# The first 512 tokens loaded by feature blocks beside weight pieces, and the first 32 matmuls run block by block

## The chip, the cores and the metric

The kernel runs on one core of one Trainium2 chip. The metric is device time in microseconds; the median of three runs of the kernel before is 504.48 (504.27 to 505.07).

## The reference

Two attention branches share one input x (1 x 2048 x 1024, bf16). Each projects it with a weight wqkv (1024 x 3072) into q, k and v of 32 heads of 32, and its result with wo (1024 x 1024). Branch A is linear attention; branch B attends to 8 earlier tokens at distances 0, 2, ..., 14. A sigmoid gate mixes the two for each token:

```
x = A_x
g = sigmoid((x * gate_w).sum(-1))
a: q,k,v = x @ A_wqkv;  phi(t) = where(t > 0, t + 1, exp(t)) + 1e-6
   o = phi(q) (phi(k)^T v) / (phi(q) sum(phi(k)));   a = o @ A_wo
b: q,k,v = x @ B_wqkv;  o = softmax over 8 dilated positions;  b = o @ B_wo
out = g * a + (1 - g) * b
```

The change touches only the start of the first product, the values of branch B: v = x @ B_wqkv[:, 2048:3072].

## The kernel before, in words

Everything goes through a planner. `P.op` (L79) records an operation with its engine, an estimated cost, a priority and the tiles that it reads and writes. `schedule` (L120) orders each engine's queue by list scheduling with these costs, and `emit` (L202) writes the queues out with the semaphore waits that the tiles demand. `plan` (L1223) is run six times, each pass choosing the PSUM banks by the pass before. So the order on each engine is fixed before the chip runs, and each queue is worked strictly in that order.

x is kept transposed in SBUF as xT, 128 partitions x 8 feature blocks x 2048 tokens. `load_x` (L1292) brings one tile of 128 tokens with all 1024 features by a transposing DMA from SP's queue. `load_w` (L1297) brings rows of a weight half (512 columns), in pieces of one or more blocks of 128 rows.

The first stage computes branch B's values, which are the first useful work of the kernel. Its loads are issued in L1306 to L1314: tile 0 on SP; the first half's weights in four pieces of two row blocks, two from ScalarE's (ACT) queue and two from SP's; tiles 1, 2, 3; the second half's weights in four pieces; then the other tiles in between the stores. The loop at L1368 takes four tiles at a time, first with the first half of the weights, then with the second. For each tile and half, `group` (L1320) issues eight matmuls of 128x128 by 128x512 that sum over the features into one PSUM bank, out of seven that rotate; tile 0 does so in four steps of two blocks, each of which waits only for its own weight piece. `move` (L1352) copies the bank to SBUF on ACT or VectorE (DVE), and a store takes it to HBM (L1377). The stage has 256 matmuls; behind them come the gate's product (L1392), k and q of branch B, and the rest, all on TensorE (PE) in one queue.

Ahead of the first useful matmul stand warm-up matmuls (L1363) on a zeroed tile `warm` into the eighth bank. They use no input data. In the kernel before they are nine of 512 columns, and VectorE zeroes the tile (L1272). GpSimd (POOL) sets up the constants, ident first (L1252).

Of the kernel before, what the change touches and what calls it, by code (L numbers as in the profile page):

```python
# [9 lines left out]
BF16 = mybir.dt.bfloat16  # L10
# [1092 lines left out]
def build_kernel(nc, A_x, A_wqkv, A_wo, B_x, B_wqkv, B_wo, gate_w, out):  # L1103
    del B_x
    S = A_x.shape[1]
    NT = S // 128
    HS = S // 2
    x2 = A_x[0].rearrange("(m e) d -> e m d", e=2)
# [5 lines left out]
    def SB(shape, dtype, name, at=None):  # L1114
        n = SZ[dtype]
        for d in shape[1:]:
            n *= d
        if at is None:
            at = base[0]
            base[0] += (n + 31) // 32 * 32  # L1120
        uid[0] += 1
        h = nc.alloc_sbuf_tensor_at("%s_%d" % (name, uid[0]), list(shape), dtype, offset=at)
        return Tile("S", h, at, list(shape), dtype)
# [28 lines left out]
    banks = [Bank(i) for i in range(8)]  # L1152
# [6 lines left out]
    def hb(p0, p1, half):  # L1159
        return [("H%d" % half, p0, p1, None)]  # L1160

    xT = SB([128, 8, S], BF16, "xT")
    qT = SB([128, 8, S], BF16, "qT")
    kT = SB([128, 8, S], BF16, "kT")
    ws = [SB([128, 8, 1024], BF16, "w%d" % i) for i in range(4)]
# [16 lines left out]
    mx4 = SB([128, 4], F32, "mx4")  # L1182
    mx1 = SB([1, 4], F32, "mx1")
    flag = SB([1, 1], I32, "flag")
    warm = SB([128, 512], BF16, "warm")
    er = Ring([SB([128, 512], BF16, "e%d" % i) for i in range(3)])

    ph = base[0]
# [25 lines left out]

    FILL = 0.2
    PVLAG = 3
    WARM = 9
    PASSES = 6
    mm = lambda n: max(n / 2400.0, 0.0267) + 0.0025
    act = lambda n: 0.19 + n / 1200.0  # L1220
    dps = lambda n: 0.14 + n / 960.0

    def plan(seen):  # L1223

        P = Prog(nc, nc.alloc_semaphore)
# [23 lines left out]
        def C(eng, fn, cost, writes, reads=()):  # L1249
            return P.op(eng, fn, cost, reads=reads, writes=writes, prio=-1)  # L1250

        C("pool", lambda e: e.memset(ident[:], 0.0), 0.2, [ident.all()])  # L1252
        C("pool", lambda e: e.affine_select(out=ident[:], in_=ident[:], compare_op=ALU.not_equal, fill=1.0, base=0,
                                            pattern=[[-1, 128]], channel_multiplier=1), 0.3, [ident.all()], [ident.all()])
# [14 lines left out]
        C("pool", lambda e: e.memset(kvbd[:], 0.0), 0.9, [kvbd.all()])  # L1269
        C("pool", lambda e: e.memset(zbd[:], 0.0), 0.9, [zbd.all()])  # L1270

        C("dve", lambda e: e.memset(warm[:, :], 0.0), 0.15, [warm.all()])  # L1272
        for m in mx[0:2]:
            C("dve", lambda e, m=m: e.memset(m[:, :], 0.0), 0.2, [m.all()])

# [12 lines left out]
        Bw = B_wqkv.rearrange("(dc p) f -> p dc f", p=128)  # L1288
# [3 lines left out]
        def load_x(t, prio):  # L1292
            e_, r = t // 8, t % 8
            return P.op("sp", lambda e: e.dma_start_transpose(xT[:, :, t * 128:(t + 1) * 128], x2[e_, r * 128:(r + 1) * 128, :]),  # L1294
                        1.5, writes=[xT.part((0, 8), (t * 128, (t + 1) * 128))], prio=prio, chan="x%d" % t, lat=1.3)

        def load_w(slot, half, src, c0, prio, d0=0, d1=8, eng="sp", after=()):  # L1297
            n = d1 - d0
            return P.op(eng, lambda e: e.dma_start(ws[slot][:, d0:d1, half * 512:half * 512 + 512], src[:, d0:d1, c0:c0 + 512]), 0.4 + 0.2 * n,  # L1299
                        writes=[ws[slot].part((d0, d1), (half * 512, half * 512 + 512))], prio=prio, chan="w%d_%d_%d" % (slot, half, d0), lat=0.55 * n, after=after)  # L1300
# [2 lines left out]
            with nc.allow_non_contiguous_dma(reason="tiny gate_w transposed load"):  # L1303
                return e.dma_start(gw[:, :], gate_w.rearrange("(dc p) -> p dc", p=128))

        load_x(0, 0)  # L1306
        load_w(0, 0, Bw, 2048, 0.1, 0, 2, "act")
        load_w(0, 0, Bw, 2048, 0.2, 2, 4, "act")
        load_w(0, 0, Bw, 2048, 0.3, 4, 6)
        load_w(0, 0, Bw, 2048, 0.4, 6, 8)  # L1310
        for t in range(1, NT):
            load_x(t, 3 + t)
        for d in range(0, 8, 2):
            load_w(0, 1, Bw, 2560, 6.1 + 0.1 * d, d, d + 2)  # L1314
# [3 lines left out]
        main = Pool(banks[0:7])  # L1318

        def group(bank, lhs, rhs, reads, lo=0, hi=8):  # L1320
            def fn(e):
                last = None
                for dc in range(lo, hi):
                    last = e.matmul(bank.ap(), lhs(dc), rhs(dc), start=(dc == 0), stop=(dc == 7))  # L1324
                return last
            return P.op("pe", fn, (hi - lo) * mm(512), reads=reads, writes=[bank.iv])
# [13 lines left out]
        def x_tile(t):  # L1340
            return (lambda dc: xT[:, dc, t * 128:(t + 1) * 128]), xT.part((0, 8), (t * 128, (t + 1) * 128))

        def x_chunk(u):
            return (lambda dc: xT[:, dc, u * 512:(u + 1) * 512]), xT.part((0, 8), (u * 512, (u + 1) * 512))

        def w_half(slot, half):
            return (lambda dc: ws[slot][:, dc, half * 512:half * 512 + 512]), ws[slot].part((0, 8), (half * 512, half * 512 + 512))

        def w_cols(slot, j):
            return (lambda dc: ws[slot][:, dc, j * 128:(j + 1) * 128]), ws[slot].part((0, 8), (j * 128, (j + 1) * 128))  # L1350

        def move(dst, src, n, bank, reg, scale=None, reads=()):  # L1352

            if scale is None:
                fd = lambda e: e.tensor_copy(dst, src())  # L1355
                fa = lambda e: e.activation(dst, src(), ACT.Copy)  # L1356
            else:
                fd = lambda e: e.tensor_scalar(dst, src(), scale, None, op0=ALU.mult)
                fa = lambda e: e.activation(dst, src(), ACT.Copy, scale=scale)  # L1359
            P.op("any", {"act": fa, "dve": fd}, {"act": act(n) + (0.1 if reads else 0.0), "dve": dps(n)}, reads=[bank.iv] + list(reads), writes=[reg])  # L1360

        for i in range(WARM):
            P.op("pe", lambda e: e.matmul(banks[7].ap(), warm[:, 0:128], warm[:, :], start=True, stop=True), 0.43, reads=[warm.all()], writes=[banks[7].iv], prio=-1)  # L1363


        early = {(2, 0): (1, 0, Bw, 1024, 21), (4, 1): (2, 0, Bw, 0, 22), (7, 1): (1, 1, Bw, 1536, 23), (10, 1): (2, 1, Bw, 512, 24),
                 (12, 1): (3, 0, Aw, 1024, 25), (14, 1): (3, 1, Aw, 1536, 26)}
        for t, half in [(4 * b + i, half) for b in range(NT // 4) for half in range(2) for i in range(4)]:  # L1368
            vt, vs = vst.next()
            xs, xr = x_tile(t)  # L1370
            bank = main.next()
            w, wr = w_half(0, half)
            step = 2 if t == 0 else 8
            for d in range(0, 8, step):
                o = group(bank, xs, w, [xr, ws[0].part((d, d + step), (half * 512, half * 512 + 512))], d, d + step)
            move(vt[:, :], bank.ap, 512, bank, vt.all())
            P.op("sp", lambda e, t=t, vt=vt, half=half: e.dma_start(vB_hbm[t * 128:(t + 1) * 128, half * 512:half * 512 + 512], vt[:, :]), 0.6, reads=[vt.all()],  # L1377
                 writes=[hb(t * 128, (t + 1) * 128, half)], chan="vst%d" % vs, lat=0.5, prio=5)
            if (t, half) in early:
                load_w(*early[t, half], after=[o])  # L1380
# [28 lines left out]
        main = Pool(banks[0:4])  # L1409
# [78 lines left out]
        for e_ in range(2):  # L1488
            if True:
                for j in range(8):  # L1490
                    for isq in range(2):
                        for u in (2 * e_, 2 * e_ + 1):
                            bank = main.next()
                            w, wr = w_cols(1 + isq, j)
                            xs, xr = x_chunk(u)
# [37 lines left out]
        for t in range(NT):  # L1533
            pkt, _ = pk.next()
            azt, _ = az.next()
            xs, xr = x_tile(t)
            for r in range(4):
                bank = main.next()
                w, wr = w_half((3, 0)[r // 2], r % 2)
# [16 lines left out]
        main = Pool(banks)  # L1556
# [109 lines left out]
        for t in range(NT):  # L1666
# [4 lines left out]
            for f0, f1 in parts:  # L1671
                bank = main.next()
                n = f1 - f0

                def fn(e, t=t, bank=bank, f0=f0, f1=f1):
# [8 lines left out]
                    reads=[bank.iv, gm.all(), tgt.part((i0, i1), (c0, c0 + 128))], writes=[o_.part((f0, f1))])  # L1684
                if t == NT - 1 or f1 == 1024:
                    c = f0 if t == NT - 1 else 0
                    P.op("sp", lambda e, e_=e_, r=r, o_=o_, c=c, f1=f1: e.dma_start(out2[e_, r * 128:(r + 1) * 128, c:f1], o_[:, c:f1]), 0.5,
                         reads=[o_.part((c, f1))], chan="out%d_%d" % (os_, c), lat=1.0)
# [8 lines left out]
    for _ in range(PASSES):  # L1697
        got = plan(seen)
        seen = got[2]
        if best is None or got[0].span < best[0].span:  # L1700
            best = got
    P, flag_op = best[:2]
# [22 lines left out]
def bass_gated_mix__linear_attn_block__sliding_local_dilated__prompt_kernel(nc, A_x, A_wqkv, A_wo, B_x, B_wqkv, B_wo, gate_w, out):  # L1725
    return build_kernel(nc, A_x, A_wqkv, A_wo, B_x, B_wqkv, B_wo, gate_w, out)
# [28 lines left out]
```

## Time and profile before

| | |
|---|---|
| three runs | 505.07, 504.48, 504.27 us |
| span of the profiled execution | 502.5 us |
| median less that span | 1.98 us |
| PE busy | 488.5 us (97%) |
| first warm-up matmul, first useful matmul | 1.25 us, 6.08 us |
| gate's product begins | 62.11 us |
| x and weight loads in the first 11 us on SP | 0.80 to 10.65 us |

The span runs from the first to the last instruction of one profiled execution; the run's time is measured from outside and is longer. All times in the profile count from the start of the span. A row of the timeline gives start, length, engine, line, operation, output and input, the number of instructions merged, and in brackets the idle time before with what ended it. SPq and ACTq are the issues of DMAs on those engines' queues, which are not the transfers themselves; the time to landing is from the issue to the last piece of data. "PEld" is the weight load of a matmul. Stretch rows give, after the stretch and its length, the busy time of PE, PEld, DVE, ACT and POOL with counts, the granted clock, the mean share of the 16 DMA engines, and GB/s.

### The profile page before, as it was taken

To read this page: it belongs to the slowest core of one execution; us is meant where nothing else is said; L and a number is where in the kernel's file an instruction comes from. 1 tells how busy PE (TensorE), PEld (TensorE's weight loads), DVE (VectorE), ACT (ScalarE), POOL (GpSimd) and SP (SyncE) were. 2 spreads that over 40 slices of the span, in tenths; PEclk is the share of its full clock that TensorE was granted. 3 is DMA by queue.
4 is the path that set the end of the run, shared out by engine and by line. 5 is a ranking of instruction groups with operands and counts; after the bars stand their busy time and mean duration, and the time that the engine had idled before them with its cause. 6 is when DMAs were issued, how large, how long until landed. Compare 5 with 4: busy or idle time off the path is not lost.

```text
span 502.5 us, 11582 instructions
## 1 busy us (share of the span) xinstructions
PE 488.5 (97%) x5190; PEld 232.6 (46%) x5257; DVE 264.6 (53%) x456; ACT 192.9 (38%) x335; POOL 6.6 (1%) x30
## 2 busy tenths in 40 slices
PE   8999999999999999999999999999999999999996
PEld 2444444444454444544544545444444444444443
DVE  3112235556667676454555464678776563234443
ACT  1111111111354454655554555479864543100000
POOL 5000000000000000000000000000000000000000
PEclk9999999999999999999999999999999999999999
DMA  8999990000024060100010100500000000011222
GB/s 222 207 204 314 353 270 1 1 0 1 12 86 139 22 198 27 34 23 23 23 39 21 33 1 3 170 0 1 0 2 0 2 0 1 1 43 64 83 78 73
DMA packets 47410, 34.92 MB, mean 69 GB/s; under 512 B 22261, under 2 KB 43125, under 8 KB 47354
## 3 DMA queue, kind: packets, MB, share of 16 engines
q1 hardware_dynamic: 46810, 33.59, 23.6%
q8 instruction: 43, 0.70, 0.6%
q10 hardware_dynamic: 544, 0.52, 0.4%
q14 instruction: 13, 0.11, 0.1%
HBM read 21.51 MB, written 8.40 MB: 60 GB/s over the span
## 4 chain that ended last, share of the span: by engine, by line
PE 95%; issue 2%; DMA 1%; ACT 1%; SPq 0%; DVE 0%
PE ps_all L1324 76%; PE ps_all L1677 11%; PE ps_all L1427 2%; PE ps_all L1447 2%; PE ps_all L1602 1%; PE ps_all L1452 1%; PE ps_all L1523 1%; DMA xT<-in_A_x_dram 1%; PE ps_all L1580 1%; ACT ra L1604 0%; PE ps_all L1392 0%; SPq L1294 0%; SPq L1299 0%; ACT e L1333 0%; ACT ra L1605 0%
## 5 line engine op out<-in xcount | busy, mean ns | idle before, releaser
L1324 PE MATMUL ps_all<-w,xT 128*128 128x512 bf16 x922 | 207.8, 379 | 5.6 <-issue 4.0
L1324 PE MATMUL ps_all<-xT,w 128*128 128x512 bf16 x747 | 169.2, 379 | 2.5 <-issue 1.9
L1324 PEld LDWEIGHTS ps_all<-w,xT 128*128 128x128 bf16 x960 | 91.3, 98 | 110.3 <-issue 1.7
L1324 PEld LDWEIGHTS ps_all<-xT,w 128*128 128x128 bf16 x768 | 73.9, 98 | 88.8 <-ACT ra L1604 0.6
L1677 PE MATMUL ps_all<-w,qT 128*128 128x512 bf16 (+1 forms) x259 | 55.2, 373 | 0.3
L1677 PEld LDWEIGHTS ps_all<-w,qT 128*128 128x128 bf16 x264 | 25.8, 98 | 29.7
L1335 DVE TENSOR_SCALAR e<-e 128x512 bf16<-128x512 bf16 x64 | 18.4, 291 | 38.9 <-ACT e L1331 25.3
L1355 DVE CAST vst<-ps_all 128x512 bf16<-128x512 f32 x15 | 10.4, 691 | 42.7 <-PE ps_all L1324 42.7
L1433 ACT ACTIVATE E<-ps_all 128x1824 bf16<-128x1824 f32 (+1 forms) x18 | 30.4, 1687 | 3.1 <-PE ps_all L1427 2.0
L1331 ACT ACTIVATE e<-ps_all 128x512 bf16<-128x512 f32 x32 | 19.1, 597 | 31.6 <-PE ps_all L1324 30.8
L1333 ACT ACTIVATE e<-ps_all 128x512 bf16<-128x512 f32 x32 | 19.2, 601 | 29.3 <-PE ps_all L1324 27.8
L1681 DVE SCALAR_TENSOR_TENSOR o<-ps_all,gm,xT 128x512 bf16<-128x512 f32 (+1 forms) x25 | 18.2, 729 | 23.0 <-PE ps_all L1677 22.8
L1280 DVE TENSOR_TENSOR mx<-mx,kT 128x1024 bf16<-128x1024 bf16 x32 | 20.7, 688 | 16.9 <-ACT kT L1356 16.8
L1280 DVE TENSOR_TENSOR mx<-mx,qT 128x1024 bf16<-128x1024 bf16 x32 | 20.7, 688 | 16.7 <-ACT qT L1359 16.6
L1356 ACT ACTIVATE vst<-ps_all 128x512 bf16<-128x512 f32 x17 | 10.1, 597 | 47.8 <-PE ps_all L1324 47.8
L1436 DVE TENSOR_TENSOR E<-E,msk 128x1824 bf16<-128x1824 bf16 (+1 forms) x18 | 19.8, 1100 | 14.5 <-ACT E L1433 14.5
L1462 DVE TENSOR_TENSOR qT<-ps_all,L 128x456 bf16<-128x456 f32 (+1 forms) x36 | 21.1, 624 | 7.7 <-ACT L L1461 7.7
L1359 ACT ACTIVATE qT<-ps_all 128x512 bf16<-128x512 f32 x15 | 9.0, 597 | 37.0 <-PE ps_all L1324 37.0
L1337 DVE SCALAR_TENSOR_TENSOR pk<-ps_all,e 128x512 bf16<-128x512 f32 x32 | 22.0, 688 | 0.8
L1604 ACT ACTIVATE ra<-ps_all,eps 128x512 f32<-128x512 f32 x32 | 21.5, 688 | 2.2 <-PE ps_all L1602 2.0
L1356 ACT ACTIVATE az<-ps_all 128x512 bf16<-128x512 f32 x19 | 11.4, 600 | 27.6 <-PE ps_all L1324 27.6
L1356 ACT ACTIVATE kT<-ps_all 128x512 bf16<-128x512 f32 x14 | 8.4, 597 | 35.5 <-PE ps_all L1324 35.5
(77 smaller groups left out, 336.5 us busy)
## 6 DMA issues: line engine op xcount, KB each, us to landing
w<-in_A_wqkv_dram SPq DMA_DIRECT2D x6, 1024.0 KB, 8.2
v<-vB_hbm SPq DMA_DIRECT2D x36, 128.0 KB, 2.6
vB_hbm<-vst SPq DMA_DIRECT2D x32, 128.0 KB, 4.9
w<-in_B_wqkv_dram SPq DMA_DIRECT2D x4, 1024.0 KB, 8.3
out_dram<-o SPq DMA_DIRECT2D x15, 256.0 KB, 2.0
w<-in_A_wo_dram SPq DMA_DIRECT2D x2, 1024.0 KB, 5.6
w<-in_B_wo_dram SPq DMA_DIRECT2D x2, 1024.0 KB, 6.5
w<-in_B_wqkv_dram SPq DMA_DIRECT2D x6, 256.0 KB, 4.1
```

What stands on the lines that cost most here:

```text
L1280: P.op("dve", lambda e, m=m, op=op: e.tensor_tensor(m[:, 0:n], m[:, 0:n], src, op), 0.08 + n / 1920.0, reads=[m.all(), reg], writes=[m.all()],
L1324: last = e.matmul(bank.ap(), lhs(dc), rhs(dc), start=(dc == 0), stop=(dc == 7))
L1331: P.op("act", lambda e: e.activation(e_[:, :], bank.ap(), ACT.Exp), act(512), reads=[bank.iv], writes=[e_.all()])
L1333: P.op("act", lambda e: e.activation(e_[:, :], bank.ap(), ACT.Exp, accum_out=qe[:, col:col + 1]), act(512) + 0.1, reads=[bank.iv], writes= ...
L1335: P.op("dve", lambda e: e.tensor_scalar(e_[:, :], e_[:, :], 1.0, 1e-6, op0=ALU.min, op1=ALU.add), 0.25, reads=[e_.all()], writes=[e_.all()])
L1337: P.op("dve", lambda e: e.scalar_tensor_tensor(out=dst, in0=bank.ap(), scalar=0.0, in1=e_[:, :], op0=ALU.max, op1=ALU.add), dps(512), read ...
L1356: fa = lambda e: e.activation(dst, src(), ACT.Copy)
L1433: P.op("act", lambda e: e.activation(E[:, 0:32 * nq].rearrange("p (j q) -> p j q", j=4), ps[:, 4:8, 0:8 * nq], ACT.Exp), act(32 * nq), rea ...
L1436: P.op("dve", lambda e: e.tensor_tensor(ev(), ev(), m[:, :, :].rearrange("p r q -> p (r q)")[:, None, :].to_broadcast([128, 16, 2 * nq]), ...
L1462: P.op("dve", lambda e, L=L, pb=pb, g=g: e.tensor_tensor(qT[:, 4 * g:4 * g + 4, t0 + qs:t0 + qs + 2 * nq].rearrange("p c (h q) -> p h c q" ...
L1604: P.op("act", lambda e: e.activation(R[:, :], db.ap(), ACT.Ln, bias=eps[:, :]), act(512), reads=[db.iv, eps.all()], writes=[R.all()])
L1677: last = e.matmul(bank.ap(0, f1 - f0), qT[:, dc, t * 128:(t + 1) * 128], ws[3][:, dc, f0:f1], start=(dc == 0), stop=(dc == 7))
```

## The change

The first four tiles are no longer loaded one by one. Eight transposing DMAs on SP each bring one block of 128 features of all 512 tokens; eight weight pieces of one row block each go out on ACT's queue. The first 32 matmuls (four tiles, first weight half) run block by block: one matmul for each of the four tiles, into four banks, then the next block. Tiles from 4 on, the second half's weights and all later work are issued as before. The warm-up becomes 22 matmuls of 128 columns on a 128x128 tile, which POOL zeroes as its first operation.

```diff
-    warm = SB([128, 512], BF16, "warm")
+    warm = SB([128, 128], BF16, "warm")
-    WARM = 9
+    WARM = 22
+        C("pool", lambda e: e.memset(warm[:, :], 0.0), 0.2, [warm.all()])
         C("pool", lambda e: e.memset(ident[:], 0.0), 0.2, [ident.all()])
...
-        C("dve", lambda e: e.memset(warm[:, :], 0.0), 0.15, [warm.all()])
...
-        load_x(0, 0)
-        load_w(0, 0, Bw, 2048, 0.1, 0, 2, "act")
-        load_w(0, 0, Bw, 2048, 0.2, 2, 4, "act")
-        load_w(0, 0, Bw, 2048, 0.3, 4, 6)
-        load_w(0, 0, Bw, 2048, 0.4, 6, 8)
-        for t in range(1, NT):
+        for d in range(8):
+            P.op("sp", lambda e, d=d: e.dma_start_transpose(xT[:, d:d + 1, 0:512], x2[0, 0:512, d * 128:(d + 1) * 128]), 0.75,
+                 writes=[xT.part((d, d + 1), (0, 512))], prio=0.1 * d, chan="xd%d" % d, lat=0.4)
+            load_w(0, 0, Bw, 2048, 0.1 * d + 0.05, d, d + 1, "act")
+        for t in range(4, NT):
             load_x(t, 3 + t)
...
-            P.op("pe", lambda e: e.matmul(banks[7].ap(), warm[:, 0:128], warm[:, :], start=True, stop=True), 0.43, ...
+            P.op("pe", lambda e: e.matmul(banks[7].ap(0, 128), warm[:, :], warm[:, :], start=True, stop=True), 0.11, ...
...
+        first = [main.next() for _ in range(4)]
+        for d in range(8):
+            for t in range(4):
+                o = group(first[t], x_tile(t)[0], w_half(0, 0)[0],
+                          [xT.part((d, d + 1), (t * 128, t * 128 + 128)), ws[0].part((d, d + 1), (0, 512))], d, d + 1)
         for t, half in [(4 * b + i, half) for b in range(NT // 4) for half in range(2) for i in range(4)]:
             vt, vs = vst.next()
             xs, xr = x_tile(t)
-            bank = main.next()
             w, wr = w_half(0, half)
-            step = 2 if t == 0 else 8
-            for d in range(0, 8, step):
-                o = group(bank, xs, w, [xr, ws[0].part((d, d + step), (half * 512, half * 512 + 512))], d, d + step)
+            if t < 4 and half == 0:
+                bank = first[t]
+            else:
+                bank = main.next()
+                step = 2 if t == 0 else 8
+                for d in range(0, 8, step):
+                    o = group(bank, xs, w, [xr, ws[0].part((d, d + step), (half * 512, half * 512 + 512))], d, d + step)
```

More of the change, by code (lines that the diff above doesn't have):

```diff
@@ L1362, in plan @@
         for i in range(WARM):
-            P.op("pe", lambda e: e.matmul(banks[7].ap(), warm[:, 0:128], warm[:, :], start=True, stop=True), 0.43, reads=[warm.all()], writes=[banks[7].iv], prio=-1)
+            P.op("pe", lambda e: e.matmul(banks[7].ap(0, 128), warm[:, :], warm[:, :], start=True, stop=True), 0.11, reads=[warm.all()], writes=[banks[7].iv], prio=-1)
         early = {(2, 0): (1, 0, Bw, 1024, 21), (4, 1): (2, 0, Bw, 0, 22), (7, 1): (1, 1, Bw, 1536, 23), (10, 1): (2, 1, Bw, 512, 24),
                  (12, 1): (3, 0, Aw, 1024, 25), (14, 1): (3, 1, Aw, 1536, 26)}
+        first = [main.next() for _ in range(4)]
[3 more added lines that the diff above has]
+                          [xT.part((d, d + 1), (t * 128, t * 128 + 128)), ws[0].part((d, d + 1), (0, 512))], d, d + 1)
         for t, half in [(4 * b + i, half) for b in range(NT // 4) for half in range(2) for i in range(4)]:
```

## The prediction

> **What bounds the kernel now.** The page's first part comes first: which engine has no room. Its second row is the engines' busy time; the share of the chain by engine stands further down the page.
>
> ```profile
> span 502.5 us, 11582 instructions
> ...
> PE 488.5 (97%) x5190; PEld 232.6 (46%) x5257; DVE 264.6 (53%) x456; ACT 192.9 (38%) x335; POOL 6.6 (1%) x30
> ...
> PE 95%; issue 2%; DMA 1%; ACT 1%; SPq 0%; DVE 0%
> ```
>
> TensorE (PE) is the bound from end to end. Only its 14 us without work (502.5 - 488.5) can be had without taking matmuls away. The waits of PE alone say where they are, in total, times and longest:
>
> ```profile
> PE ps_all L1324 <- issue: 5.9, 37, 0.2
> PE ps_all L1363 <- DVE warm L1272: 1.3, 1, 1.3
> PE ps_all L1324 <- DMA xT<-in_A_x_dram: 1.0, 2, 0.8
> ```
>
> The 5.9 us are gaps of at most 0.2 us, spread over the kernel. The only data that PE waits for as a matmul is xT, at the very beginning. So the change can act only there, and the chain of waits and PE's timeline show that stretch (start, length, what):
>
> ```profile
> 0.80 1.37 SPq L1294
> 2.17 0.06 issue
> ...
> 3.35 4.94 DMA xT<-in_A_x_dram
> ...
> 8.33 7.16 PE ps_all L1324 x32
> ...
> 15.55 10.74 PE ps_all L1324 x49
> ...
> 62.11 1.84 PE ps_all L1392 x32
> ```
>
> ```profile
> 1.25 4.02 PE L1363 MATMUL ps_all<-warm 128*128 128x512 bf16 x9 [1.25 <-DVE warm L1272]
> 6.08 2.06 PE L1324 MATMUL ps_all<-w,xT 128*128 128x512 bf16 x8 [0.81 <-DMA xT<-in_A_x_dram]
> 8.33 8.03 PE L1324 MATMUL ps_all<-w,xT 128*128 128x512 bf16 x35 [0.18 <-DMA xT<-in_A_x_dram]
> ```
>
> Nine idle-data matmuls run from 1.25 to 5.27. The first useful matmul starts at 6.08, when token tile 0 has landed; its eight are through at 8.14, and tile 1 lets the ninth start at 8.33. From there PE runs on: 248 matmuls until the gate's line at 62.11, so (62.11 - 8.33) / 248 = 0.217 us each. By this rate the 32nd ends at 8.33 + 24 x 0.217 = 13.54 and the 40th at 15.27. **This is the yardstick: whatever the 40th gains, the whole kernel gains**, because in the built program PE's later instructions stand in the old order, and no wait for a DMA shows behind it. The profiled execution spans 502.5 us; the median of the runs shown, 504.48, is 1.98 more, which I carry over unchanged.
>
> **Part 1: the warm-up.** Rate and zeroing, by groups and timeline:
>
> ```profile
> L1363 PE MATMUL ps_all<-warm 128*128 128x512 bf16 x9 | 4.0, 628 | 1.3 <-DVE warm L1272 1.3
> L1324 PE MATMUL ps_all<-w,xT 128*128 128x512 bf16 x43 | 10.0, 380 | 1.1 <-DMA xT<-in_A_x_dram 1.0
> ```
>
> ```profile
> 0.80 0.20 POOL L1252 MEMSET ident<- 128x128 bf16 x1 [0.29 <-POOLq L1740]
> ...
> 0.93 0.27 DVE L1272 MEMSET warm<- 128x256 uint32 x1 [0.93 <-PEq L1740]
> ```
>
> Nine warm-ups in 4.02 us, the last of them 0.628 long, start (4.02 - 0.63) / 8 = 0.424 us apart; the useful ones start 0.217 apart. PE begins at half rate and has its full rate by 6.08, which is 4.83 us after its first matmul. The zeroing moves from VectorE to the head of GpSimd's queue, where a memset of the same shape runs from 0.80 to 1.00, so PE, which began 0.05 after the old zeroing was done, starts at about 1.05. Twenty-two matmuls of 128 columns at a quarter of 0.424 take 2.33 us: over at 3.4 instead of 5.27. The constants behind it on POOL come 0.2 us later; ident and the masks serve stages behind the gate's line at 62.11, which is their cover. At the same 4.83 us after the start, full rate comes at 5.9; I take 6.0.
>
> **Part 2: the loads.** Now the issuing queues, and the landing of single transfers (the transposed tile issued at 7.17, then tile 0's, then pieces of 256 KB):
>
> ```profile
> 0.80 0.95 ACTq L1299 DMA_DIRECT2D w<-in_B_wqkv_dram  x2
> 0.80 1.37 SPq L1294 DMA_TRANSPOSE xT<-in_A_x_dram  x1
> 3.35 5.14 SPq L1294 DMA_TRANSPOSE xT<-in_A_x_dram  x3
> 8.53 2.12 SPq L1299 DMA_DIRECT2D w<-in_B_wqkv_dram  x4
> ```
>
> ```profile
> L1294 SPq DMA_TRANSPOSE xT<-in_A_x_dram x1: 1311/1311/1311, 7.2 to 7.2; - x1
> ...
> DMA to landing us min/median/max: 3.3/3.3/3.3
> ```
>
> ```profile
> L1294 SPq DMA_TRANSPOSE xT<-in_A_x_dram x1: 1368/1368/1368, 0.8 to 0.8; - x1
> ...
> DMA to landing us min/median/max: 5.1/5.1/5.1
> ```
>
> ```profile
> L1299 ACTq DMA_DIRECT2D w<-in_B_wqkv_dram x1: 433/433/433, 0.8 to 0.8; - x1
> ...
> DMA to landing us min/median/max: 2.9/2.9/2.9
> ```
>
> ```profile
> L1299 SPq DMA_DIRECT2D w<-in_B_wqkv_dram x1: 469/469/469, 10.2 to 10.2; - x1
> ...
> DMA to landing us min/median/max: 4.7/4.7/4.7
> ```
>
> ```profile
> 2.00:3.00 1.00, 1.00 (x4) 0.35 (x3) 0.28 (x1) 1.00 (x1) 1.00 (x2) 1.00 0.64 211
> 7.00:8.00 1.00, 1.00 (x5) 0.15 (x3) 0.43 (x2) 0.00 (x0) 0.50 (x2) 1.00 1.28 287
> 12.00:13.00 1.00, 1.00 (x6) 0.49 (x5) 0.69 (x1) 0.00 (x0) 0.00 (x0) 1.00 1.04 341
> ```
>
> A 128x1024 transpose holds SP 1.31 us; a plain load holds its queue 0.45. A 512x128 block is half the elements, and no row shows one. Its issue lies between 0.45 (nothing but the fixed part) and 1.31 (nothing saved); half of the part above a plain load gives 0.45 + 0.43 = 0.88, which I take. With the 0.06 between two issues in the chain above, eight blocks hold SP from 0.80 to 0.80 + 8 x 0.94 = 8.3. Before, four tiles and two weight pieces held it until 8.53: SP gains almost nothing.
>
> The transfers: transposes alone moved 287 GB/s (7 to 8 us), weights alone 341 (12 to 13). A 128 KB block is 0.46 us of DMA, a 128 KB piece 0.38. Eight of each are 6.7 us; with data flowing from about 2.0 they are in at 8.7 at the earliest. One pair per 0.84 us of DMA, and one block per 0.94 of SP, feed four matmuls that take 0.87: about in step.
>
> First landing: a quiet tile took 3.3 from issue, 2.0 of it after the issue; of these 0.91 are its own 256 KB. A quiet block: 0.80 + 0.88 + 2.0 - 0.46 = 3.2. Tile 0, beside ACT's weights, took 5.1, that is 1.7 longer after its issue: 4.9 for a block. ScalarE now issues eight pieces in a row (8 x 0.48, until 4.6), so the company stays; but a block is half a tile. I take the middle, **4.0**. ScalarE's table load slips behind them, to some 6 us; its first eviction is due after 11.
>
> PE's own path: from 4.0 to 6.0 at half rate 4.7 matmuls, the other 35.3 at 0.217 take 7.7: the 40th ends at 13.7, **1.6 us earlier**. A late block holds up all of PE's queue; in step with the blocks it should cost a few tenths at most.
>
> **Part 3: what is late next.** The 33rd to 40th matmul need the second half of the weights, 1 MB in four pieces, still on SP behind the blocks. First issue 8.3. The last piece landed 4.7 after its issue before, which from 8.3 + 1.65 gives 14.65. The other end: an empty queue landed 256 KB in 2.9, and three more pieces follow at 0.77 (256 KB at 341 GB/s): 8.3 + 2.9 + 2.3 = 13.5. The tile load that was in front of them before is gone and the blocks are nearly through, so I take 13.5. Two matmuls wait for that piece: the 40th ends at 13.93, later than PE's own 13.7. So the weights set the gain: 15.27 - 13.93 = **1.34 us**. With 14.65 it would be 0.2.
>
> Nothing: the order of evictions (four banks come free within 0.9 us of each other, ACT and DVE are idle then, and seven banks rotate); tiles 4 and 5 on SP, due at the 65th matmul near 19; the gate's small operations on DVE, a few places later.
>
> **The sum.** 504.48 - 1.34 = **503.1 us**. What a measurement here can tell from no change is about 0.2%, 1.0 us.
>
> **Rivals.**
>
> *Full rate comes late* (chance 0.25). In the profile the rate doubled after 4.02 us of nearly unbroken matmuls; now there are 2.33, a gap of some 0.6, and then useful ones. If between 3.39 (last warm-up's start after the first) and 4.83 us of unbroken work is needed, counted from 4.0, full rate comes at 7.4 to 8.8. The 40th then ends at 7.4 + 32 x 0.217 = 14.3 up to 8.8 + 28.7 x 0.217 = 15.0: gain 0.2 to 0.9, 503.6 to 504.2. Against it: the old gap of 0.81 us did not keep the first useful matmuls from full rate. These rows show rates and nothing of the gate: the granted clock reads 1.00 from 2 to 3 us, when PE runs at half rate.
> The Trainium skill ("TensorE: Matmul & The Clock Gate", Part 1, What's actually happening) says the array starts at half clock and is released by a free-running window of about 3.4 us that was busy. By that page this warm-up is shorter than one window and the release falls, estimated, anywhere from 4.5 to 7.9, so single runs would differ by up to 1.7 us. No run here shows the window's phase.
>
> *The blocks don't issue faster than whole tiles* (0.11), the slow side. At 1.31 + 0.06 each, SP is free at 11.8 instead of 8.3, and the second half lands at 11.8 + 5.2 = 17.0: the 40th ends at 17.4, 2.2 us later than before, 506.6. It decides from an issue of 1.05 us, where the last piece lands at 14.85. For it: a tile under load held SP far longer, 5.14 for three. Against it: these queued behind each other.
>
> *All goes early* (0.12). Issue at half of 1.31, 0.66: SP free at 6.6; then DMA limits, 2.0 + 6.7 + 3.1 = 11.8 for 3 MB and some 0.7 to land: 12.5, the 40th at 12.9, if PE starts at 3.2 and has its rate by 4.5. Gain 2.3, 502.1.
>
> That the change doesn't do what it says has no room: the built program issues eight blocks and eight pieces and runs the first 32 matmuls from four banks.
>
> **How the numbers follow.** Forecast 0.50 (a few hundredths of it gain less than 1.0), early 0.12, late rate 0.25, slow issue 0.11, the rest mishaps. Faster 0.58, same 0.31, slower 0.11. The range runs from the early case, 502.1, to where slow issue begins to cost, 505.2 (an issue of 1.14); that leaves about 0.15 out.
>
> **What to look for.** Line of the block load: 0.8 to 0.95 us each, and SP at the second half's weights near 8.3. First useful matmul near 4.0, four at a time, half rate until 6. PE waiting on w, not xT, around the 37th to 39th matmul; the 40th at 13.9. Past 16 us every stretch of PE as long as before. I am wrong if a block's issue is over 1.05, if half rate lasts past 7.4, or if PE's later idle time changes.

## The result, and the profile after

The changed kernel takes 506.76 us (median of 5 runs, 506.07 to 507.75), the kernel before 504.48 (504.27 to 505.07): a ratio of 1.0043, 95% interval [1.003, 1.0056]. It is slower by 2.3 us. The forecast was 503.1 with a range to 505.2; the rival on the slow side had given 506.6. The profiled execution spans 505.2 us (its run: 506.95), 2.7 more than before.

The page of the changed kernel shows first that nothing changed in what PE has to do:

```profile
span 505.2 us, 11626 instructions
...
PE 488.8 (97%) x5203; PEld 233.9 (46%) x5270; DVE 264.2 (52%) x455; ACT 192.7 (38%) x335; POOL 6.8 (1%) x31
```

PE is busy 0.3 us longer, so 2.4 of the 2.7 us are waiting. The waits of PE, in total, times and longest:

```profile
PE ps_all L1323 <- issue: 6.0, 38, 0.2
PE ps_all L1323 <- DMA xT<-in_A_x_dram: 2.7, 2, 1.5
...
PE ps_all L1323 <- DMA w<-in_B_wqkv_dram: 0.7, 1, 0.7
```

The small gaps are the same 6 us. The wait for xT has grown from 1.0 to 2.7, and there is a new one for w. The chain of waits tells in order what stood in the way (start, length, what):

```profile
0.80 1.24 SPq L1307
...
9.91 1.26 SPq L1307
...
11.21 0.58 SPq L1299
...
12.86 4.80 DMA w<-in_B_wqkv_dram
...
17.71 8.59 PE ps_all L1323 x39
...
64.94 1.84 PE ps_all L1399 x32
```

Eight issues of a block, one behind the other, fill SP's queue from 0.80 to 11.17. Only then does SP issue the second half's weights. The last of their four pieces goes out at 12.86 and lands 4.80 later. Two matmuls wait for it, so the 40th ends at 17.66 + 2 x 0.216 = 18.1, where it had ended at 15.27. From there on nothing differs: the gate's product starts at 64.94 instead of 62.11, 2.83 later, and what follows takes 440.3 us in this profile and 440.4 before (span less the gate's start).

PE's and SP's timelines of the same stretch:

```profile
1.06 2.53 PE L1362 MATMUL ps_all<-warm 128*128 128x128 bf16 x22 [1.06 <-POOL warm L1252]
5.13 4.67 PE L1323 MATMUL ps_all<-w,xT 128*128 128x512 bf16 x12 [1.54 <-DMA xT<-in_A_x_dram]
10.95 5.35 PE L1323 MATMUL ps_all<-w,xT 128*128 128x512 bf16 x23 [1.15 <-DMA xT<-in_A_x_dram]
17.02 3.23 PE L1323 MATMUL ps_all<-w,xT 128*128 128x512 bf16 x13 [0.72 <-DMA w<-in_B_wqkv_dram]
```

```profile
0.80 10.37 SPq L1307 DMA_TRANSPOSE xT<-in_A_x_dram  x8
11.21 2.12 SPq L1299 DMA_DIRECT2D w<-in_B_wqkv_dram  x4
```

The first useful matmul comes at 5.13, one microsecond sooner than before. The twelve matmuls of blocks 0 to 2 take 4.67 us, mostly at half rate (starts 0.427 apart until 8.3). Block 3 lets PE wait until 10.95, and then the second half's weights until 17.02 and 17.71.

The stretches of two microseconds give the third change; the last two columns are the share of the DMA engines and GB/s. The changed kernel, then the kernel before:

```profile
4.00:6.00 2.00, 0.87 (x3) 0.35 (x4) 1.20 (x3) 0.57 (x1) 1.82 (x10) 1.00 1.15 165
6.00:8.00 2.00, 1.98 (x6) 0.52 (x5) 0.62 (x3) 0.71 (x1) 1.57 (x7) 1.00 1.19 223
8.00:10.00 2.00, 1.72 (x7) 0.31 (x4) 0.00 (x0) 0.00 (x0) 0.00 (x0) 1.00 1.27 173
```

```profile
4.00:6.00 2.00, 1.27 (x3) 0.15 (x1) 1.06 (x3) 0.00 (x0) 1.83 (x10) 1.00 1.12 278
6.00:8.00 2.00, 1.91 (x8) 0.63 (x8) 0.62 (x3) 0.00 (x0) 1.43 (x7) 1.00 1.21 308
8.00:10.00 2.00, 1.82 (x9) 0.80 (x9) 0.00 (x0) 0.60 (x1) 0.00 (x0) 1.00 1.01 220
```

The DMA engines are no less busy than before, but in these six microseconds they move 165 to 223 GB/s, 187 on average, where they had moved 220 to 308, 269 on average. Three things are therefore suspect: SP's issues, the slow transfers beside two queues, and the late doubling of PE's rate.

### The profile page after: what moved, and what is told of

Same layout as the page of the kernel before. It is cut to its first block, busy times and chain, and to the rows that moved or that the text cites. A ratio compares the mean times of both kernels' runs of the same rounds, so it can differ in the third digit from the quotient of the medians.

```text
span 505.2 us, 11626 instructions
## 1 busy us (share of the span) xinstructions
PE 488.8 (97%) x5203; PEld 233.9 (46%) x5270; DVE 264.2 (52%) x455; ACT 192.7 (38%) x335; POOL 6.8 (1%) x31
## 3 DMA queue, kind: packets, MB, share of 16 engines
q10 hardware_dynamic: 1152, 1.05, 1.1%
## 4 chain that ended last, share of the span: by engine, by line
PE 94%; SPq 2%; issue 2%; DMA 1%; ACT 1%; DVE 0%
PE ps_all L1323 74%; PE ps_all L1684 11%; PE ps_all L1434 2%; SPq L1307 2%; PE ps_all L1454 2%; PE ps_all L1609 1%; PE ps_all L1459 1%; PE ps_all L1530 1%; DMA w<-in_B_wqkv_dram 1%; PE ps_all L1587 1%; ACT ra L1611 0%; PE ps_all L1399 0%; SPq L1299 0%; ACT e L1332 0%; ACT ra L1612 0%
```

## The experiments

**Theory**: a transpose costs SP some 1.25 us whatever it moves, and eight of them keep the second half's weights back; this alone makes the loss. **Rivals**: the DMA engines are the limit, because blocks and pieces from two queues slow each other; or the short warm-up lets PE run at half rate too long. Each run was taken beside runs of the kernel before on the same chip, whose medians are 504.30 to 504.57 us, and ratios are against those.

| run | us, median | ratio, 95% interval |
|---|---|---|
| the change | 506.76 | 1.0043 [1.003, 1.0056] |
| second half's weights from ACT | 509.22 | 1.0103 [1.0079, 1.0126] |
| short warm-up alone, in before | 505.67 | 1.0024 [1.0012, 1.0035] |
| the change with the long warm-up | 507.05 | 1.0059 [1.0046, 1.0072] |
| four blocks of 256 features | 506.99 | 1.0043 [1.0028, 1.0058] |
| the change without first-half weights | 507.19 | 1.0049 [1.0032, 1.0065] |
| that, with four blocks | 504.30 | 0.9993 [0.9982, 1.0004] |
| before, first-half weights all from ACT | 506.07 | 1.0029 [1.0016, 1.0042] |
| four blocks, long warm-up | 506.23 | 1.0037 [1.0023, 1.005] |
| four blocks, long warm-up, tile 4 held | 506.14 | 1.0027 [1.0016, 1.0039] |
| the change, tile 4 held | 507.51 | 1.0054 [1.0035, 1.0073] |
| four blocks, long warm-up, one queue | 504.59 | 1.0005 [0.9996, 1.0014] |

### What one transpose costs its queue

```diff
 # kernel before; tiles 4 to 15 in other shapes (the loops over d are left out)
+load_xs(4, 4, d, 4, 7 + 0.1 * d)    # 512 tokens x 512 features, twice
+load_xs(8, 4, d, 2, 11 + 0.1 * d)   # 512 x 256, four times
 load_x(12, 15)                      # 128 x 1024
+load_xs(13, 1, d, 4, 16 + 0.1 * d)  # 128 x 512, twice
+load_xs(14, 1, d, 2, 17 + 0.1 * d)  # 128 x 256, four times
+load_xs(15, 1, d, 1, 18 + 0.1 * d)  # 128 x 128, eight times
```

> The kernel before, with tiles 4 to 15 loaded in other shapes: tiles 4 to 7 as two transposes of 512 tokens x 512 features, tiles 8 to 11 as four of 512 x 256, tile 12 as before (128 x 1024), tile 13 as two of 128 x 512, tile 14 as four of 128 x 256, tile 15 as eight of 128 x 128. It measures how long one issue holds SP. If the issue is a fixed price per transpose: 1.23 to 1.3 us for every shape. If it goes by elements above a fixed part (the prediction's step): 0.88 for 128 x 512, 0.66 for 128 x 256, 0.56 for 128 x 128, 2.2 for 512 x 256. If it goes by rows of the source: 512-row shapes longer than 128-row ones at the same features, and 128 x 128 about a quarter of 512 x 128.

SP's timeline in this kernel (start, length): a 512 x 256, the 128 x 1024, a 128 x 512, a 128 x 256 and a 128 x 128.

```profile
18.14 1.22 SPq L1316 DMA_TRANSPOSE xT<-in_A_x_dram  x1
...
27.56 1.23 SPq L1294 DMA_TRANSPOSE xT<-in_A_x_dram  x1
...
29.93 1.21 SPq L1316 DMA_TRANSPOSE xT<-in_A_x_dram  x1
...
33.67 1.17 SPq L1316 DMA_TRANSPOSE xT<-in_A_x_dram  x1
...
45.53 1.10 SPq L1316 DMA_TRANSPOSE xT<-in_A_x_dram  x1
```

An eighth of the elements saves a tenth of the price: 1.10 against 1.23 us. For these shapes the price is nearly per transpose, as expected for a fixed price. Some issues took longer: the two of 512 x 512, right behind the second half's weights, held SP for 6.56 us, and the second of the 512 x 256 for 2.55. I read that as earlier transfers backing up into the queue; a 512 x 512 on a quiet queue was not measured. The run took 505.36 us, a single one. SP had 21 transposes behind tile 3 instead of 12, so the next weights went out at 59.41 instead of 38.60, and PE waited 0.9 us for them.

### Is the number of issues enough for the loss?

Here the first half's weights are nearly taken out, so that almost nothing runs beside the transposes (the first 512 columns of the values then have no meaning); then the number of issues is halved.

```diff
 # the change, weights of the first half: block 0 only, used for all eight
-            load_w(0, 0, Bw, 2048, 0.1 * d + 0.05, d, d + 1, "act")
+            if d == 0:
+                load_w(0, 0, Bw, 2048, 0.05, 0, 1, "act")
```

> The changed kernel with only block 0 of the first half's weights loaded, and used in place of the other seven (the values of the first 512 columns are then of no meaning); 0.9 MB less for the DMA engines, SP's queue as it was. Theory (SP's issues set the end): the blocks land sooner after their issues, but the second half's weights still go out at 11.2 and land some 3.2 to 4.8 later, so the 40th ends at 16.5 to 18: 505.3 to 506.7. Rival (DMA engines are the limit): 0.9 MB at 190 GB/s is 4.7 us, which would bring all loads forward: 504 or less.

```diff
 # the same, four blocks of 256 features
-        for d in range(8):
-            P.op("sp", lambda e, d=d: e.dma_start_transpose(xT[:, d:d + 1, 0:512], x2[0, 0:512, d * 128:(d + 1) * 128]), 0.75,
+        for d in range(0, 8, 2):
+            P.op("sp", lambda e, d=d: e.dma_start_transpose(xT[:, d:d + 2, 0:512], x2[0, 0:512, d * 128:(d + 2) * 128]), 1.3,
```

> The run without the first half's weights (only block 0 of them is loaded and used for all eight, so the values of the first 512 columns have no meaning), with four transposes of 512 x 256 in place of eight of 512 x 128. Beside that run it differs in the number of issues on SP alone, and nothing runs beside the transposes. Theory (each transpose costs SP about 1.25 us whatever it moves, and this alone was enough for the loss): SP is free at 6.0 instead of 11.2, the second half lands by 11 to 12, and the time falls by 2 to 4 us to 503.0 to 505.0 (the upper end if the rate doubles late). Rival (the issues are not the limit): it stays at 507.2.

Eight blocks: 507.19 us, no faster than the change though 0.9 MB less is to be moved, and a little above the expected range. Four blocks: 504.30, as expected. The chain and one stretch of the first, and SP's timeline of the second:

```profile
12.86 4.73 DMA w<-in_B_wqkv_dram
...
17.64 8.59 PE ps_all L1324 x39
```

```profile
7.00:9.00 2.00, 1.42 (x6) 0.42 (x6) 0.43 (x2) 0.00 (x0) 0.64 (x3) 1.00 0.42 95
```

```profile
0.80 5.38 SPq L1307 DMA_TRANSPOSE xT<-in_A_x_dram  x4
6.23 2.12 SPq L1299 DMA_DIRECT2D w<-in_B_wqkv_dram  x4
```

With eight blocks the last weight piece goes out at 12.86 and lands at 17.59, within 0.1 us of the change, although the blocks alone had kept the DMA engines less than half busy (0.42 between 7 and 9 us). With four, SP is free at 6.2, and 2.9 us are gone (507.19 - 504.30). The theory stands as far as it goes: the eight issues alone are enough for the whole loss.

### Halving the issues in the whole kernel

```diff
-        for d in range(8):                      # blocks of 128 features
+        for d in range(0, 8, 2):                # blocks of 256; ACT's eight weight pieces as they were
```

> The changed kernel with four transposes of 512 tokens x 256 features instead of eight of 512 x 128; the same bytes, weight pieces, matmul order and warm-up. Theory (a transpose costs SP some 1.2 us whatever its shape, so eight of them keep the second half's weights off the queue until 11.2): SP is free at about 6.0, the second half's pieces land by 15 to 16 instead of 17.66, and the 40th matmul ends near 16: 505.2 (504.4 to 505.8). Rival (the DMA engines are the limit: moving the second half's pieces ahead in time, as on ScalarE's queue, only pushes the blocks back): 506.7 or more.

It took 506.99 us, as much as the change: the theory's 505.2 was missed, the rival's 506.7 or more came true. So the theory is not the whole: lift this limit with the weights in place, and another stands right behind it. PE's timeline of this kernel, and SP's:

```profile
5.36 14.86 PE L1324 MATMUL ps_all<-w,xT 128*128 128x512 bf16 x55 [1.77 <-DMA xT<-in_A_x_dram]
```

```profile
0.80 7.75 SPq L1307 DMA_TRANSPOSE xT<-in_A_x_dram  x4
8.60 2.16 SPq L1299 DMA_DIRECT2D w<-in_B_wqkv_dram  x4
```

Four issues took 7.75 us, not the 5.38 of the kernel without the pieces: beside them, transfers back up into the queue. And PE, busy from 5.36 with short gaps, ran at half rate until 10.1 in this execution. The profile is of the shortest of its six runs (505.68 of 505.68 to 507.49), so the median run lost more than it shows. Two more limits had to be told apart.

### The late rate

```diff
 # kernel before, with the change's warm-up
-    WARM = 9                 # of 512 columns, zeroed by DVE
+    WARM = 22                # of 128 columns, zeroed by POOL
```

> The kernel before with the change's warm-up alone: 22 matmuls of 128 columns, zeroed by GpSimd, loads and order as before. Theory (the loads set the loss, the warm-up has little part in it): PE's idle gap before the first useful matmul grows from 0.8 to some 2.5 us, the rate doubles later (8.3 in the changed kernel), and what this costs is what half rate lasts beyond 6.1, less the waits that it covers: 504.5 to 505.4. Rival (the late doubling makes the loss): 506 or more, the whole of the change's 2.3 us.

```diff
 # the change, with the old warm-up
-    WARM = 22
+    WARM = 9
```

> The changed kernel with the old warm-up: nine matmuls of 512 columns on a 128x512 tile that VectorE zeroes. Theory (the second half's weights behind SP's issues set the end): the rate doubles near 5.7, the first blocks are worked faster and PE waits longer for the next ones, and the total stays: 506.5 to 506.9. Rival (the late doubling makes the loss): back by up to 1.2 us or more, 505.5 or less.

The short warm-up alone costs the kernel before 1.1 us (505.67 against 504.57), a little above the expected range and below the rival's 506: first useful matmul at 5.82, starts 0.427 apart until about 11. The chain has 27 matmuls in 8.53 us there, and 32 in 7.16 in the kernel before:

```profile
5.82 8.53 PE ps_all L1324 x27
```

The long warm-up gives the change nothing back (507.05). Its profile is of the shortest of its five runs (505.99). In it PE has its full rate from 6.9 us and then waits 1.27 and 0.67 us for blocks, so the earlier rate went into waiting. The gate's product starts 1.0 us sooner than in the change's profile, but that is the landing of the last weight piece, issued at 12.86 in both:

```profile
12.86 3.81 DMA w<-in_B_wqkv_dram
```

It took 3.81 us here and 4.80 there. So the late rate is a real price in the kernel before, and hidden in the change behind the loads.

### Two queues at once

```diff
 # kernel before
-        load_w(0, 0, Bw, 2048, 0.3, 4, 6)
-        load_w(0, 0, Bw, 2048, 0.4, 6, 8)
+        load_w(0, 0, Bw, 2048, 0.3, 4, 6, "act")
+        load_w(0, 0, Bw, 2048, 0.4, 6, 8, "act")
```

> The kernel before with all four pieces of the first half's weights issued from ScalarE's queue instead of two from each. Theory (two queues at once slow each other): tile 0 lands later than 6.0, at 6.5 to 7.5, tile 1 later than 8.3, and the DMA engines move some 200 GB/s between 3 and 7 us instead of 270 to 340; the time is 504.6 to 506. Rival (no such slowing): SP saves two issues, tiles 1 to 3 come up to 1 us sooner, 503.8 to 504.3.

It took 506.07 us, 1.5 more than before, although SP has two issues less. Tile 0 landed where it did, the other tiles later. PE's timeline and stretches of this kernel, then the stretches of the kernel before:

```profile
6.08 2.74 PE L1324 MATMUL ps_all<-w,xT 128*128 128x512 bf16 x6 [0.81 <-DMA xT<-in_A_x_dram]
9.80 6.43 PE L1324 MATMUL ps_all<-w,xT 128*128 128x512 bf16 x29 [0.97 <-DMA w<-in_B_wqkv_dram]
```

```profile
5.00:7.00 2.00, 1.19 (x4) 0.37 (x4) 0.48 (x3) 0.00 (x0) 1.77 (x9) 1.00 1.19 260
7.00:9.00 2.00, 1.83 (x5) 0.31 (x3) 0.43 (x2) 0.00 (x0) 0.50 (x2) 1.00 1.25 199
```

```profile
5.00:7.00 2.00, 1.19 (x6) 0.47 (x6) 0.48 (x3) 0.00 (x0) 1.77 (x9) 1.00 1.15 315
7.00:9.00 2.00, 1.81 (x9) 0.47 (x8) 0.43 (x2) 0.60 (x1) 0.50 (x2) 1.00 1.10 247
```

The seventh matmul waited for a weight piece of ACT's queue until 9.80; before, it started within 1.5 us of the first (eight were through at 8.14). PE was also at half rate until 9.5 in this execution, with the warm-up of the kernel before; but the piece landed only at 9.75, so the rate did not set this wait. The expected place of the delay (tile 0) was wrong, its cause is seen: while both queues had work, the engines were no less busy and moved less, and the first 2 MB were in by 11.5 us instead of 10.5. A block of 128 features is not itself slower to move than a tile: alone, blocks moved 95 GB/s at a share of 0.42 (above), tiles 287 at 1.28, which is the same for each unit of the share.

```diff
 # the change; the second half's weights behind the eight pieces on ACT
-            load_w(0, 1, Bw, 2560, 6.1 + 0.1 * d, d, d + 2)
+            load_w(0, 1, Bw, 2560, 0.9 + 0.01 * d, d, d + 2, "act")
```

> The changed kernel, with the second half's four weight pieces issued from ScalarE's queue right behind its eight, instead of from SP's behind the eight blocks. Theory (eight block issues of 1.25 us each hold SP until 11.2, and the second half's weights, issued behind them, set the end of the 40th matmul): the pieces are issued by about 8 and have landed by 14 to 15, the blocks' last landing at 12.9 is then the limit, the 32nd matmul ends near 13.8 and the 40th near 15.5, close to the kernel before: 504.7 us (504.2 to 505.3). Rival (the DMA engines are the limit, since blocks and pieces together move only some 190 GB/s): the 3 MB end when they did, the 40th stays near 18: 506.7. Rival (the late doubling of PE's rate): PE's rate doubles as late as before, and most of the loss stays: 506 or more.

It took 509.22 us, far from the theory's 504.7 and from the first rival's 506.7. The other rival's "506 or more" holds in number alone: PE was at half rate until 13.9, but after that it still waited 1.45 us for a block. The pieces do go out by 8.0, so the theory's chain is cut, but now twelve pieces of ACT run beside the eight blocks, and the blocks wait. From the chain, block 5 from its issue to landing, and PE's last wait for xT:

```profile
7.30 8.59 DMA xT<-in_A_x_dram
```

```profile
15.94 24.35 PE L1323 MATMUL ps_all<-w,xT 128*128 128x512 bf16 x109 [1.45 <-DMA xT<-in_A_x_dram]
```

Block 5 is there at 15.94; in the change it was being worked at 10.95 + 8 x 0.216 = 12.7. All 3 MB are in by 16.5, sooner than in the change (17.66), but the blocks, which are needed first, come last. Freeing SP by means of the other queue makes it worse.

### One queue, four blocks

```diff
 # four blocks of 256 features, weights in pieces of 256 rows, old warm-up
+            load_w(0, 0, Bw, 2048, 0.1 * d - 0.15, d, d + 2, "act" if d == 0 else "sp")
```

> Four blocks of 256 features; the first half's weights in four pieces of 256 KB, the first from ScalarE's queue and the other three from SP's, each behind the block before it, so that the two kinds of transfer follow each other in one queue instead of running beside each other; the old warm-up. Theory (beside the fixed price of an issue, transposes and plain loads from two queues slow each other: some 190 GB/s together, against 290 and 340 one after the other; and PE falls back to half rate when it waits long between blocks): SP is free at 8, the blocks land at about 4, 6, 8 and 9.5, PE has no long gap, the second half lands by 12.7, and the 40th matmul ends at 13.8: 503.0 (502.6 to 503.9), ahead of the kernel before. Rival (the total of bytes or the clock is the limit, not the mixing): the 40th at 15.5 to 16.5, 504.7 to 505.7.

```diff
 # four blocks of 256 features, weights in eight pieces on ACT, old warm-up
+        for d in range(0, 8, 1):
             load_w(0, 0, Bw, 2048, 0.1 * d + 0.05, d, d + 1, "act")
```

> Four blocks of 256 features, weights from ScalarE's queue in eight pieces as in the change, and the old warm-up; it is the run with four blocks, with the warm-up alone exchanged. Theory (with two queues the second block lands late, 8.9 to 10, so PE waits 1.5 to 3 us behind the first eight matmuls and may lose its rate again): 505.5 to 506.5, little better than 506.99. Rival (the late rate made the whole rest of the loss): 504.5 or less.

With the pieces on ACT 506.23 us, with one queue 504.59: 1.6 us for the same bytes and the same four issues of blocks, though pieces of 256 KB instead of 128 come with it. PE's timelines, first with ACT's pieces, then with one queue:

```profile
5.87 1.90 PE L1324 MATMUL ps_all<-w,xT 128*128 128x512 bf16 x8 [0.71 <-DMA xT<-in_A_x_dram]
8.75 1.90 PE L1324 MATMUL ps_all<-w,xT 128*128 128x512 bf16 x8 [0.97 <-DMA xT<-in_A_x_dram]
11.22 9.02 PE L1324 MATMUL ps_all<-w,xT 128*128 128x512 bf16 x41 [0.58 <-DMA xT<-in_A_x_dram]
```

```profile
5.07 6.09 PE L1323 MATMUL ps_all<-w,xT 128*128 128x512 bf16 x24
11.72 8.50 PE L1323 MATMUL ps_all<-w,xT 128*128 128x512 bf16 x38 [0.56 <-DMA xT<-in_A_x_dram]
```

With one queue PE starts when the warm-up is over and has 24 matmuls done by 11.2. The chains have the block that PE waited for last (issue, time to landing): with ACT's pieces the third, with one queue the fourth.

```profile
3.55 7.63 DMA xT<-in_A_x_dram
```

```profile
7.00 4.67 DMA xT<-in_A_x_dram
```

In this pair it is the order of arrival that differs, more than the rate. With ACT's pieces the third block lands at 11.18 and the fourth at 11.83; with one queue they land at 9.21 and 11.67. The last piece of the second half lands at 14.93 and 14.82, and between 3 and 11 us the engines move 224 and 235 GB/s. So at 11.2 PE still has 16 matmuls of the first 32 ahead of it with ACT's pieces, and eight at 11.7 with one queue.

Yet one queue is no faster than the kernel before, and the 503.0 that was expected of it was missed, while its rival's 504.7 to 505.7 came close: the fourth block comes at 11.7, and the gate's product starts at 62.09, as before at 62.11. The early start is given back, because x's first 512 tokens and both halves, 3 MB, are not in sooner than before (14.82 against 14.84). No version here beats the kernel before.

### Holding tile 4 back

```diff
 # the change: tiles from 4 on wait for the first 32 matmuls (the next weight load is moved back, not shown)
+                for t_ in range(4, NT):
+                    load_x(t_, 3 + t_, after=[o])
```

> The changed kernel with tile 4 and those behind it issued only after the first 32 matmuls (and the next weight load, due at the 256th matmul, a little later), so that no transpose runs beside the second half's weight pieces. In the changed kernel the last two pieces landed at 16.98 and 17.66, while tile 4's packets ran from 15.6. Theory (the collision is part of the loss): the last piece lands near 16.0 and the 40th ends at 16.4 instead of 18.1: 505.1 (504.7 to 505.6). Rival (the issue at 11.2 to 12.9 alone): 506.5.

> Three mends together: four blocks of 256 features, the old warm-up of nine matmuls of 512 columns, tile 4 held back until the first 32 matmuls are through. If issue, late rate and collision are the whole loss: second half landed by 14 to 14.5, the 40th ends at 14.5 to 15.0, which is 0.3 to 0.8 ahead of the kernel before: 503.8 to 504.3. If the DMA engines beside two queues remain slow: 505 or more.

Neither settles what tile 4's transpose costs the weights beside it. Held back in the change, 507.51 us: no gain, and PE waited for xT again at 30.66, so the edit added a wait of its own. With the other two mends, 506.14, against 506.23 without holding. The last weight piece landed 4.1 us after its issue with tile 4 held in the change and 4.8 without, but 3.8 in the change with the long warm-up, where tile 4 is not held.

Both profiles show something else; each is of the longest of its kernel's runs (509.59 and 507.39). PE's timeline and stretches with tile 4 held in the change, then a wait and a stretch of the kernel with all three mends; the column before the last two is the granted clock:

```profile
4.22 1.53 PE L1321 MATMUL ps_all<-w,xT 128*128 128x512 bf16 x4 [0.63 <-DMA xT<-in_A_x_dram]
7.10 1.04 PE L1321 MATMUL ps_all<-w,xT 128*128 128x512 bf16 x4 [1.34 <-DMA xT<-in_A_x_dram]
9.69 20.30 PE L1321 MATMUL ps_all<-w,xT 128*128 128x512 bf16 x78 [1.55 <-DMA xT<-in_A_x_dram]
```

```profile
9.00:12.00 3.00, 2.31 (x6) 0.84 (x7) 0.00 (x0) 0.00 (x0) 0.00 (x0) 0.50 1.19 208
12.00:15.00 3.00, 3.00 (x9) 1.06 (x7) 0.00 (x0) 0.00 (x0) 0.00 (x0) 0.50 0.81 230
```

```profile
10.02 10.28 PE L1322 MATMUL ps_all<-w,xT 128*128 128x512 bf16 x38 [2.95 <-DMA xT<-in_A_x_dram]
```

```profile
11.00:14.00 3.00, 3.00 (x9) 1.02 (x8) 0.00 (x0) 0.00 (x0) 0.00 (x0) 0.50 1.20 290
```

With tile 4 held, PE had its full rate when it worked on block 1 (four matmuls in 1.04 us), with a wait of 1.34 us ahead of it and one of 1.55 behind it, and from 9 to 15 us it was granted half the clock: nine matmuls in three microseconds. In the other kernel a wait of 2.95 us came ahead of the fall. Working block by block, a late block can cost the rate as well as the wait. The record agrees that this is part of why these kernels differ more from run to run (506.56 to 509.59 with tile 4 held) than the kernel before: in five of them the runs with a mean granted clock below 0.998 are the longest ones (509.59 at 0.992, for one), and no run of the kernel before has less than 0.998. No experiment was made on it.

## Why the prediction was wrong

- **What bounds it, and the yardstick** held. Only the first 18 us changed, and what the 40th matmul lost (2.8 us) the profiled execution lost (2.7).
- **Part 1, the warm-up**: the start at 1.05 was right (1.06). Full rate at 6.0 was wrong: it came at 8.3 in the changed kernel's profile. The rival on it was right that it comes late, and wrong that this decides: the run with the long warm-up did not gain. In the kernel before the same warm-up costs 1.1 us, so this rival, which I gave a quarter, names a true price in the wrong place. What neither my own term nor the rival had is how far the rise to full rate moves: after the short warm-up it came between 4.6 and 13.9 us in seven profiles, after the long one between 4.1 and 9.5 in seven others. Three kernels with the same warm-up and the same first loads had it at 5.3 (tile 4 held in the change), 8.3 (the change) and 13.9 (second half from ACT). By the Trainium skill ("TensorE: Matmul & The Clock Gate", Part 1, What's actually happening) the array must be busy for a free-running window of some 3.4 us. The spread is in line with a window that runs freely, but no run here shows its phase. Only two of the seven after the short warm-up lie between the 4.5 and 7.9 that I estimated from it, and the rise at 4.1 came 2.8 us after PE's first matmul.
- **Part 2, the issue of a block: the step that failed.** I had the two ends right, 0.45 and 1.31, and took 0.88 by halving what lies above a plain load. It is 1.24 to 1.26, and the shapes show that elements hardly count. Eight times 0.37 are 3 us on SP: free at 11.2, not 8.3. The rival gave this a chance of 0.11 and 506.6 us. That its number lies so near to 506.76 is partly luck: it had SP free 0.6 us too late and the second half in 1.25 too soon after that.
- **Part 2, the transfers**: 6.7 us for 2 MB by the rates of transposes alone and of weights alone. The last block, issued at 9.91, landed 3.0 us later, at 12.9; that is SP's pace in part, but with four blocks and ACT's pieces PE still waited for xT until 11.22. Rates seen one kind at a time (287 and 341 GB/s) were added as if they held side by side, where the two together moved 165 to 223.
- **Part 2, first landing**: 4.0 expected, 5.13 in this profile, 4.22 to 4.39 in two others with the same first loads. A half-right step.
- **Part 3, what is late next**: right that the second half's weights set the end. The set took 17.66 - 11.21 = 6.45 us from first issue to last landing; I took 5.2, and the kernel before's own row (4.7 after the last issue) would have given 6.35. This second term was too small by 1.25 us. 2.9 us of SP and 1.25 here are the 4.2 us between 13.9 and 18.1.
- **The early case** (502.1) had no place: even with one queue, four issues and the old warm-up, the 3 MB are in no sooner than in the kernel before.

What is shown: eight issues alone are enough for the loss (507.19 against 504.30); two weight pieces moved to the second queue cost the kernel before 1.5 us; lifting the issues alone (506.99) or taking the second half's weights off SP alone (509.22) leaves the change slow. What is argued: why two queues moved less together, and how much of their price is rate and how much is the order of arrival. What stays open: what tile 4's transpose costs the weights beside it.

## What to carry to other kernels

Count DMA issues on a queue before counting bytes: a transpose cost SP 1.1 to 1.25 us whether it moved 32 KB or 256 KB, so cutting a load finer delays whatever is issued behind it. When a load is split to start the work sooner, look at the load that is needed after it: here the first matmul came 1 us sooner and the 40th 2.8 us later. And before a second queue is given work to free the first, measure with both at once how much they move and in what order it lands.

## What the runs showed of the hardware

A transpose by DMA has a nearly fixed price on a quiet queue: 1.09 to 1.13 us for 128 x 128, 1.17 for 128 x 256, 1.19 to 1.21 for 128 x 512, 1.23 to 1.37 for 128 x 1024, 1.22 to 1.27 for 512 x 256, 1.23 to 1.26 for 512 x 128. Behind other transfers it took longer, 2.55 us for a 512 x 256. A plain load of 128 to 256 KB took 0.38 to 0.64.

Transposes from SP beside plain loads from ACT moved 165 to 223 GB/s with the DMA engines' share above 1 (the change, 4 to 10 us); one kind at a time, 287 and 341 had been moved in the kernel before. The Trainium skill ("DMA: Bandwidth & Descriptors", Issuing engines are not separate DMA queues) says that DMAs of all issuing engines run on the same 16 DMA engines and interleave, so that a second queue saves only issue time. The runs agree, and add that running side by side cost time here: with two pieces moved to ACT's queue the kernel before took 1.5 us longer.

PE's granted clock can fall back to 0.50 between bursts of matmuls: it did behind waits of 1.34 and 1.55 us around a burst of 1.04 (9 to 15 us above), and behind one of 2.95. Waits of 0.97 and 0.58 us (four blocks, long warm-up) and of 1.27 and 0.67 (the change with the long warm-up) left it at 1.00. Ahead of the first rise the clock column of the profile reads 1.00 although matmuls start at half rate.
